# Four attention layers on one core: residual kept in SBUF, attention outputs stored once as float32, accumulator copy and value products reordered, other DMA steps

## The chip, the cores and the metric

The kernel runs on one core of one Trainium2 chip. The metric is the device time of one execution in microseconds (us). Three runs of the kernel before took 6309.92, 6320.90 and 6321.18 us, so the median is 6320.9 us. The profile comes from one further execution, which took 6320.79 us; its span, from the first to the last instruction in the profile, is 6319.0 us.

## The reference

```python
def _A_ref(x, wqkv, wo):                     # 32 heads of width 18, S = 2048, D = 576
    qkv = (x @ wqkv).reshape(B, S, 3, H, Dh).transpose(2, 0, 3, 1, 4)
    q, k, v = qkv[0], qkv[1], qkv[2]
    scores = jnp.einsum("bhqd,bhkd->bhqk", q, k) * (Dh ** -0.5)
    o = jnp.einsum("bhqk,bhkd->bhqd", _softmax(scores), v)
    return o.transpose(0, 2, 1, 3).reshape(B, S, D) @ wo
# _B_ref: the same with one k and one v of width 18 that all 32 heads share

x = A_x
x = x + _A_ref(_layernorm(x), A_wqkv, A_wo)
x = x + _B_ref(_layernorm(x), B_wq, B_wk, B_wv, B_wo)
x = x + _A_ref(_layernorm(x), A_wqkv, A_wo)
x = x + _B_ref(_layernorm(x), B_wq, B_wk, B_wv, B_wo)
```

All inputs and the output are float32. Where the kernel multiplies in the faster matmul format `F32R`, it splits a float32 number into a rounded part `hi` and a remainder `lo` and adds up the products of the parts (`TERMS`, 14 products for a contraction over 576).

## The kernel before

**Four layers, each in four stages.** (1) *Projection*: 8 blocks `tt` of 256 tokens. The normalized rows are transposed and split (`trans`, `split_rows`) into a tile `xt`, and `project` makes q and k, which go to DRAM (`qk_d`). (2) *Attention*, the long stage. (3) *Output projection* (`out_proj`): 16 chunks `c` of 128 tokens; `out_w` makes 28 matmuls (14 for each half of 288 columns, tile `psn`) and adds the result to the residual. (4) The normalization for the next layer, woven into (3).

**Attention** runs over groups: a group is one pair of heads `p` (16 of them) and one block `u` of 512 queries (4 of them), so 64 groups in a layer and 256 in all. A group takes 8 steps `st` of 4 slots `i`. The row maxima of a group are made first (`max_mm`: PE fills a two-bank tile `psm`, VectorE reduces it at line 439), and `LEAD` = 14 steps later come the scores again, transposed, with the maximum subtracted in the matmul (`exp_mm`: PE fills `pse`, one of three banks, and ScalarE takes the exponential into a tile `pt`), and then the products with the values (`pv_block`). `max_mm` and `exp_mm` of one slot use different halves of the PE rows. A `pv_block` of one step multiplies four `pt` tiles with the values into one PSUM bank, `oacc`; each logical product is two matmuls in the profile. In slot 1 the second half (256 columns) of the step before last is multiplied, in slot 3 the first half of the last step. The first step of a group is the exception (`pv_slot`): its first half is left out in slot 3, and all 512 columns are done in slot 1 of the next step, because `oacc` must be copied (`oc`, line 576, on ScalarE) before the next group overwrites it. The copy stands in ScalarE's order behind the exponential of slot 1.

**Work around a group.** A table `todo` says at which step each piece is issued; every engine has its own order and only waits for what it needs. For group `g`, with `b` its last step of maxima:

- The maxima are finished (`max_final`: VectorE line 528, then three small GpSimd instructions), turned (`max_store` at `b`+2: VectorE line 538, four DMAs at line 540 into `m_d`) and laid as two rows into the q tile (`max_rows` at `b`+5: two DMAs at line 544). The scores of the group need these rows.
- The sum of the exponentials comes from the copy `oc`: `o_sum` (three GpSimd instructions, lines 132 and 590), `l_part` (line 595: two DMAs, `lt`), `l_inv` (line 599, VectorE), `l_out` (line 602, to `r_d`), `l_rows` (line 607, `rb`), `o_mul` (GpSimd line 612, then two more that make `hi` and `lo`, lines 132 and 615), `o_out` (line 621, four DMAs into `o_d`).

All DMAs are issued in one order by SyncE (SP), and SP waits at each for what it depends on. With 8 steps in a group, pieces of several groups fall on the same step; where they do, the older group's come first. Counted modulo 8, the phases are: `max_store` 1, `max_rows` 4, `o_sum` 0, `l_part` 1, `l_inv` and `l_out` 4, `l_rows` 6, `o_mul` 0, `o_out` 2. So at phase 0 GpSimd gets `o_mul` of an older group ahead of `o_sum`; at phase 1 SP gets `l_part` ahead of `max_store`; at phase 4 it gets `l_out` ahead of `max_rows`.

**Output projection.** The residual lies in DRAM (`x_d`, or the input in layer 0). `load_res` brings each chunk into a tile `xr`, `out_w` adds into it, and a DMA (line 297) stores it; `load_x` loads it again for the next layer's normalization. `out_rows` loads `hi` and `lo` of the attention outputs for 256 tokens straight into a matmul operand `ot` (three buffers). What is left of the last groups' steps is run between the chunks (`run_tail`, two steps a chunk).

Of the kernel before, what the change touches and what calls it, by code (L numbers as in the profile page):

```python
# [8 lines left out]
F32 = mybir.dt.float32  # L9
# [9 lines left out]
P = 128  # L19
# [28 lines left out]
L_AT = 4  # L48
INV_AT = 7
R_AT = 7  # L50
RB_AT = 9
MUL_AT = 11
O_AT = 13
# [10 lines left out]
XT = 3  # L64
# [3 lines left out]
def tile_kernel(ctx: ExitStack, tc: tile.TileContext, A_x, A_wqkv, A_wo, B_x, B_wq, B_wk, B_wv, B_wo, out):  # L68
# [24 lines left out]
    wsm = cst.tile([P, 10, D], F32R, name="wsm")  # L93
    vbuf = cst.tile([P, NCH * H * (DH + 1)], F32, name="vbuf")
# [8 lines left out]
    o_d = dram.tile([2, D, S], F32, name="o_d")  # L103
    r_d = dram.tile([H, S], F32, name="r_d")

    rbs = [cst.tile([P, 512], F32, name=f"rb{i}") for i in range(2)]
# [4 lines left out]
    for t in rbs + sums + [h_.bitcast(F32) for h_ in hls]:  # L111
        nc.gpsimd.memset(t, 0.0)
    x_d = [dram.tile([S, D], F32, name=f"x_d{i}") for i in range(2)]
# [11 lines left out]
    def ptile(name, shape=(P, 512), dt=F32):  # L125
        return pool.tile(list(shape), dt, tag="p", bufs=16, name=name)
# [87 lines left out]
    xcs, xrs = {}, {}  # L214

    def load_x(tt, src):
        for c in (2 * tt, 2 * tt + 1):
            xcs[c] = pool.tile([P, D], F32, tag="xc", bufs=4, name="xc")
            nc.sync.dma_start(xcs[c], src[c * P:(c + 1) * P, :])

    def stats(c):
        xc = xcs[c]
# [10 lines left out]
    def scaled(c, mv, rs):  # L233
        xc = xcs.pop(c)
# [14 lines left out]
    def load_res(c, src):  # L249
        if c < NCH:  # L250
            xrs[c] = pool.tile([P, D], F32, tag="xr", bufs=4, name="xr")
            nc.sync.dma_start(xrs[c], src[c * P:(c + 1) * P, :])

    def out_w(c):
        ot = ots_[c // 2][:, :, c % 2 * P:(c % 2 + 1) * P]
        for h in range(2):
            cs = slice(h * 288, (h + 1) * 288)
            nc.vector.tensor_tensor(xrs[c][:, cs], natural(ot, h, mtile), xrs[c][:, cs], op=OP.add)  # L258

    ots_, lts, rls, his = {}, {}, {}, {}  # L260
    xhs, xts = {}, {}

    def trans(c):
        tt, u = divmod(c, 2)
        if u == 0:
            xts[tt] = pool.tile([P, 9, 256], F32R, tag="xt", bufs=XT, name="xt")
# [16 lines left out]
    def out_proj(x_res_prev, x_new_prev):  # L283

        for c in range(2):
            load_res(c, x_res_prev)
        yield -1
        for c in range(NCH + 1):
            if c < NCH:
# [424 lines left out]
```

## Time and profile before

| | |
|---|---|
| median of three runs | 6320.9 us (6309.92 to 6321.18) |
| the profiled execution: time, span | 6320.79 us, 6319.0 us |
| mean granted TensorE clock over it | 0.979 |
| VectorE busy | 5323.0 us (84%) |
| ScalarE busy | 4691.3 us (74%) |
| GpSimd busy | 1815.4 us (29%) |
| moved by DMA | 359.38 MB, 57 GB/s on average |

How to read it: PE is TensorE's matmuls and PEld its weight loads, DVE is VectorE, ACT ScalarE, POOL GpSimd; SPq is SyncE's queue of DMA issues. `pse<-big` means that an instruction reads the tile `big` and writes the tile `pse`. A row of the timeline shows the start and the duration of one instruction, or of several alike that follow each other (x8), and in brackets the idle time of the engine before it with what ended it. Matmuls are pipelined: the next starts before the recorded end of the one before, so the distance of starts says more than a duration.

### The profile page before, as it was taken

To read this page: it belongs to the slowest core of one execution; us is meant where nothing else is said; L and a number is where in the kernel's file an instruction comes from. 1 tells how busy PE (TensorE), PEld (TensorE's weight loads), DVE (VectorE), ACT (ScalarE), POOL (GpSimd) and SP (SyncE) were. 2 spreads that over 40 slices of the span, in tenths; PEclk is the share of its full clock that TensorE was granted. 3 is DMA by queue.
4 is the path that set the end of the run, shared out by engine and by line. 5 is a ranking of instruction groups with operands and counts; after the bars stand their busy time and mean duration, and the time that the engine had idled before them with its cause. 6 is when DMAs were issued, how large, how long until landed. Compare 5 with 4: busy or idle time off the path is not lost.

```text
span 6319.0 us, 134168 instructions
## 1 busy us (share of the span) xinstructions
PE 6064.2 (96%) x53280; PEld 2682.3 (42%) x53280; DVE 5323.0 (84%) x5592; ACT 4691.3 (74%) x8848; POOL 1815.4 (29%) x2701
## 2 busy tenths in 40 slices
PE   9999999999899999999899999999998999999999
PEld 8533333334733333333595333333347333333335
DVE  4799999996589999999337999999964999999992
ACT  2588888887178888888425888888861788888883
POOL 2132322333123323333311332333330233332331
PEclk9999999999999999999999999999998999999998
DMA  5311111112611111011453111111126111011004
GB/s 188 93 46 36 32 36 36 33 33 60 205 48 24 24 25 23 23 25 24 142 178 87 42 35 36 34 35 36 30 75 192 46 25 25 24 25 25 22 16 129
DMA packets 348700, 359.38 MB, mean 57 GB/s; under 512 B 142776, under 2 KB 283376, under 8 KB 338352
## 3 DMA queue, kind: packets, MB, share of 16 engines
q1 hardware_dynamic: 348072, 350.81, 19.8%
q8 instruction: 419, 6.86, 0.5%
q14 instruction: 209, 1.71, 0.1%
HBM read 201.05 MB, written 145.59 MB: 55 GB/s over the span
## 4 chain that ended last, share of the span: by engine, by line
PE 55%; DVE 14%; DMA 8%; POOL 7%; ACT 7%; SPq 6%; issue 4%; POOLq 0%; DVEq 0%; ACTq 0%
PE pse L553 23%; PE oacc L570 20%; DVE mx L439 13%; PE psq L322 5%; ACT pt L556 5%; PE psn L209 4%; DMA big<-m_d 3%; PE psm L433 3%; SPq L540 2%; ACT oc L576 2%; SPq L621 1%; POOL oh L615 1%; POOL os L590 1%; POOL os L132 1%; DMA x_d<-xr 1%
## 5 line engine op out<-in xcount | busy, mean ns | idle before, releaser
L439 DVE TENSOR_REDUCE mx<-psm 128x1 f32<-128x1024 f32 x4096 | 4971.0, 1219 | 273.8 <-PE psm L433 258.5
L556 ACT ACTIVATE pt<-pse 128x512 f32<-128x512 f32 x8192 | 4428.8, 600 | 752.8 <-PE psm L433 331.1
L433 PE MATMUL psm<-big 62*128 62x512 f32 x8192 | 3065.8, 453 | 48.2 <-DVE mx L439 39.2
L553 PE MATMUL pse<-big 64*128 64x512 f32 x8192 | 3000.0, 446 | 116.4 <-DMA big<-m_d 74.8
L570 PE MATMUL oacc<-pt,vbuf 128*19 128x256 f32 (+1 forms) x30720 | 2534.9, 402 | 0.0
L553 PEld LDWEIGHTS pse<-big 64*128 64x128 f32 x8192 | 1233.6, 185 | 1981.1 <-ACT pt L556 1897.1
L433 PEld LDWEIGHTS psm<-big 62*128 62x128 f32 x8192 | 1232.2, 187 | 150.5 <-DVE mx L439 130.9
L570 PEld LDWEIGHTS oacc<-pt,vbuf 128*19 128x19 f32 x30720 | 523.1, 97 | 1380.1 <-issue 1375.8
L530 POOL TENSOR_SCALAR neg<-mm 128x8 f32<-128x8 f32 x256 | 50.9, 199 | 3263.8 <-DVE mm L528 3263.8
L322 PE MATMUL psq<-xt,big 128*128 128x256 f32 (+1 forms) x3136 | 427.8, 297 | 26.0 <-DVE ev L332 17.3
L322 PEld LDWEIGHTS psq<-xt,big 128*128 128x128 f32 (+1 forms) x3136 | 407.7, 201 | 44.1 <-DVE ev L332 20.3
L326 ACT ACTIVATE ev<-psq 128x512 fp32r<-128x512 f32 (+2 forms) x148 | 73.2, 495 | 446.4 <-PE psq L322 401.4
L612 POOL TENSOR_TENSOR os<-os,rb 96x512 f32<-96x512 f32 x256 | 327.5, 1279 | 113.2 <-DMA rb<-r_d 101.6
L132 POOL TENSOR_SCALAR os<-oc 32x512 f32<-32x512 f32 x512 | 316.0, 617 | 66.2 <-ACT oc L576 28.2
L615 POOL TENSOR_TENSOR oh<-os,oh 96x512 fp32r<-96x512 f32 x256 | 327.9, 1281 | 21.4
L590 POOL TENSOR_TENSOR os<-os,oc 96x512 f32<-96x512 f32 x256 | 327.8, 1280 | 21.4
L209 PE MATMUL psn<-wsm,ot 128*128 128x288 f32 x1792 | 263.6, 310 | 49.4 <-DVE xr L258 49.4
L258 DVE TENSOR_TENSOR xr<-psn,xr 128x288 f32<-128x288 f32 x128 | 56.4, 454 | 270.2 <-PE psn L209 124.1
L209 PEld LDWEIGHTS psn<-wsm,ot 128*128 128x128 f32 x1792 | 256.0, 201 | 58.4 <-DVE xr L258 55.7
L332 DVE TENSOR_TENSOR ev<-psq,ev 128x512 fp32r<-128x512 f32 (+2 forms) x120 | 69.7, 591 | 199.8 <-ACT ev L326 187.0
L193 ACT ACTIVATE xt<-ps 128x512 fp32r<-128x512 f32 x64 | 38.2, 596 | 215.7 <-PE ps L201 214.9
L576 ACT ACTIVATE oc<-oacc 128x512 f32<-128x512 f32 x256 | 154.4, 603 | 23.0 <-PE oacc L570 23.0
(52 smaller groups left out, 1239.7 us busy)
## 6 DMA issues: line engine op xcount, KB each, us to landing
big<-qk_d SPq DMA_DIRECT2D x180, 432.0 KB
qk_d<-ev SPq DMA_DIRECT2D x192, 256.0 KB
o_d<-oh SPq DMA_DIRECT2D x1024, 36.0 KB
ot<-o_d SPq DMA_DIRECT2D x64, 512.0 KB
qk_d<-ev SPq DMA_DIRECT2D x240, 128.0 KB
rb<-r_d SPq DMA_DIRECT2D x512, 36.0 KB
m_d<-tr SPq DMA_DIRECT2D x1024, 2.0 KB
x_d<-xr SPq DMA_DIRECT2D x48, 288.0 KB
```

Of the source, the lines that this page charges most:

```text
L132: eng.tensor_scalar(dst, src, 1.0, 0.0, op0=OP.mult, op1=OP.add)
L209: nc.tensor.matmul(ps, lhs[:, xc, :], wsm[:, wc, h * 288:(h + 1) * 288], start=i == 0, stop=i == len(TERMS) - 1)
L322: nc.tensor.matmul(ps[:n, k, :], w[:, wc, :n], xt[:, xc, :], start=j == 0, stop=j == len(TERMS) - 1)
L433: nc.tensor.matmul(ps[:, i % 2], q[b:b + KM, c0:c0 + P], k[b:b + KM, kb * 512:(kb + 1) * 512], start=True, stop=True)
L439: nc.vector.reduce_max(mxs[p, u][:, a * 4 + qc, j // 8:j // 8 + 1], ps.rearrange("p a t -> p (a t)"), axis=AX.X)
L553: nc.tensor.matmul(e, k[r:r + KE, kc * P:(kc + 1) * P], q[r:r + KE, u * 512:(u + 1) * 512], start=True, stop=True)
L556: nc.scalar.activation(pt, e, AF.Exp, scale=SCALE)
L570: nc.tensor.matmul(oacc[j:j + DH + 1, cs], v[:, kc, 2 * p + a if is_a else 0, :], pts[p, u, i][:, cs], start=kc < 2, stop=kc >= 14 and hal ...
L576: nc.scalar.activation(oc, oacc, AF.Copy)
L590: nc.gpsimd.tensor_tensor(t[:96], t[:96], oc[:96], op=OP.add)
L612: nc.gpsimd.tensor_tensor(t[:96], t[:96], rbs[u % 2][:96], op=OP.mult)
L615: nc.gpsimd.tensor_tensor(lo[:96], t[:96], hi.bitcast(F32)[:96], op=OP.subtract)
```

## The change

1. **Residual.** One tile `xo` of 16 x 576 floats a partition holds the whole residual. It is loaded once from the input in layer 0; `stats`, `scaled` and `out_w` work on slices of it. `load_res`, the tiles `xc` and `xr`, the DRAM tensors `x_d`, their stores and the reloads are gone. In the last layer each chunk is stored to the output from `xo`. The next layer's first normalization steps move from chunks 4 and 5 to chunks 3 and 4.
2. **Attention outputs.** `o_mul` is one GpSimd instruction instead of three, and `o_out` two DMAs instead of four: `o_d` holds float32. `out_rows` loads it into three tiles from the pool of `pt`, and the new `out_t` makes `hi` (copies on ScalarE, for the first block on VectorE) and `lo` (subtractions on VectorE) in the operand `ot`. `ot` and `xt` have two buffers instead of three, the pool of `pt` 15 instead of 16, `rb` one instead of two.
3. **Copy and value products.** In the step in which a group's last value product is issued, the exponential of slot 1 is issued after the copy `oc` instead of before it. `pv_slot` is gone: each step's products are done in halves, the first step of a group too, whose first half now stands in slot 3, half a step behind the copy. The flag `start` is set on the first half alone.
4. **Order.** New distances, and with them the phases modulo 8: `o_sum` stays at 0, `l_part` goes to 2, `l_inv` and `l_out` to 5, `l_rows` to 0, `o_mul` to 2, `o_out` to 4. `max_store` (1) and `max_rows` (4) stay.

```diff
-L_AT = 4
-INV_AT = 7
-R_AT = 7
-RB_AT = 9
-MUL_AT = 11
-O_AT = 13
+L_AT = 5
+INV_AT = 8
+R_AT = 8
+RB_AT = 11
+MUL_AT = 13
+O_AT = 15
...
+    xo = cst.tile([P, NCH, D], F32, name="xo")
...
     def out_rows(tt):
         ts = slice(tt * 256, tt * 256 + 256)
-        ots_[tt] = pool.tile([P, 9, 256], F32R, tag="xt", bufs=XT, name="ot")
-        ot = ots_[tt].bitcast(F32)
+        ors[tt] = t = [ptile("o", (P, 2, 256)) for _ in range(3)]
         for i in range(2):
-            nc.sync.dma_start(ot[:, 5 * i:5 * i + 4], o_d[i, :512, ts].rearrange("(c p) t -> p c t", p=P))
-            nc.sync.dma_start(ot[64 * i:64 * i + 64, 4], o_d[i, 512:, ts])
+            nc.sync.dma_start(t[i], o_d[256 * i:256 * i + 256, ts].rearrange("(c p) t -> p c t", p=P))
+            nc.sync.dma_start(t[2][64 * i:64 * i + 64, 0], o_d[512:, ts])
+
+    def out_t(tt, hi):
+        ots_[tt] = ot = pool.tile([P, 9, 256], F32R, tag="xt", name="ot")
+        ot_f = ot.bitcast(F32)
+        t = ors.pop(tt)
+        for i in range(2):
+            copy(hi, ot[:, 2 * i:2 * i + 2], t[i])
+            nc.vector.tensor_tensor(ot[:, 5 + 2 * i:7 + 2 * i], t[i], ot_f[:, 2 * i:2 * i + 2], op=OP.subtract)
+        copy(hi, ot[:, 4], t[2][:, 0])
+        nc.vector.tensor_tensor(ot[64:, 4], t[2][64:, 0], ot_f[64:, 4], op=OP.subtract)
 
     def out_w(c):
         ot = ots_[c // 2][:, :, c % 2 * P:(c % 2 + 1) * P]
         for h in range(2):
             cs = slice(h * 288, (h + 1) * 288)
-            nc.vector.tensor_tensor(xrs[c][:, cs], natural(ot, h, mtile), xrs[c][:, cs], op=OP.add)
+            nc.vector.tensor_tensor(xo[:, c, cs], natural(ot, h, mtile), xo[:, c, cs], op=OP.add)
...
+    def out_proj(last):
+
+        for c in range(NCH):
+            tt = c // 2
+            if c >= OUT_AHEAD:
+                run_tail(TAIL)
+            if c % 2 and tt + 2 < 8:
+                out_rows(tt + 2)
+            out_w(c)
+            if c % 2 == 0 and tt + 1 < 8:
+                out_t(tt + 1, nc.scalar)
+            if last:
+                nc.sync.dma_start(y_out[c * P:(c + 1) * P, :], xo[:, c])
+            yield c
...
-            pt = ptile("pt")
-            nc.scalar.activation(pt, e, AF.Exp, scale=SCALE)
-            pts[p, u, i] = pt
+
+            def finish():
+                pt = pts[p, u, i] = ptile("pt")
+                nc.scalar.activation(pt, e, AF.Exp, scale=SCALE)
+            return finish
...
-            cs = slice(0, 512) if half is None else slice(half * 256, half * 256 + 256)
+            cs = slice(half * 256, half * 256 + 256)
...
-                                 start=kc < 2, stop=kc >= 14 and half == 1)
+                                 start=kc < 2 and half == 0, stop=kc >= 14 and half == 1)
...
         def o_mul(p, u):
             t = sums[u % 2]
-            nc.gpsimd.tensor_tensor(t[:96], t[:96], rbs[u % 2][:96], op=OP.mult)
-            hi, lo = his[p, u] = [pool.tile([P, 512], F32R, tag="oh", name="oh") for _ in range(2)]
-            copy(nc.gpsimd, hi[:96], t[:96])
-            nc.gpsimd.tensor_tensor(lo[:96], t[:96], hi.bitcast(F32)[:96], op=OP.subtract)
+            nc.gpsimd.tensor_tensor(t[:96], t[:96], rb[:96], op=OP.mult)
...
-        for i in range(XT - 1):
-            at(b - 8 + 2 * i + 4 * (i // 2), out_rows, i)
+        at(b - 5, out_rows, 0)
+        at(b - 2, out_t, 0, nc.vector)
+        at(b - 1, out_rows, 1)
...
             for i in range(4):
+                held = None
                 if 0 <= se < ns:
-                    exp_mm(*divmod(se // STEPS, 4), se % STEPS * 4 + i, st >= ns)
+                    held = exp_mm(*divmod(se // STEPS, 4), se % STEPS * 4 + i, st >= ns)
+
+                    if i != 1 or (se - 2) % STEPS != STEPS - 1:
+                        held()
+                        held = None
...
                 if i == 1:
-                    pv_slot(se - 2, 1)
+                    pv_block(se - 2, 1)
                 elif i == 3:
-                    pv_slot(se - 1, 0)
+                    pv_block(se - 1, 0)
+                if held:
+                    held()
```

More of the change, by code (lines that the diff above doesn't have):

```diff
@@ L281, in run_tail @@
                     f(*args)
[L283 to L289, printed above, removed]
[L290 to L303 removed]
+    def out_proj(last):
[11 more added lines that the diff above has]
+            yield c
+        assert not tail and not ors
+    load_x(0)
     for layer in range(4):
         is_a = layer % 2 == 0
[L306 to L307 removed]
         if is_a:
@@ L484, in tile_kernel @@
                     load_wsm(c, A_wqkv[:, 2 * D:])
-            if tt < 5:
-                load_x(tt + 3, x_res)
+            if layer == 0 and tt < 5:
+                load_x(tt + 3)
             gs = groups if tt < 6 else first
@@ L676, in tile_kernel @@
                 tail = [todo.pop(n, []) for n in range(ns + LEAD + L_AT + 1, ns + LEAD + O_AT)]
-                outs = out_proj(x_res, x_new)
-                next(outs)
+                outs = out_proj(layer == 3)
             elif ns <= se < ns + OUT_AHEAD:
```

73 lines of the change are left out of this document (23 added, 50 removed).

## The prediction

> **What bounds the kernel now.** I read the page first, then the timeline of a few steps in the long stage, then the waits, then the distances of the copies `oc`, which count groups, and last the four output projections.
>
> ```profile
> PE 6064.2 (96%) x53280; PEld 2682.3 (42%) x53280; DVE 5323.0 (84%) x5592; ACT 4691.3 (74%) x8848; POOL 1815.4 (29%) x2701
> L439 DVE TENSOR_REDUCE mx<-psm 128x1 f32<-128x1024 f32 x4096 | 4971.0, 1219 | 273.8 <-PE psm L433 258.5
> ```
>
> Three engines look full, so the page alone does not say which one sets the pace. The timeline does:
>
> ```profile
> 1006.93 0.50 PE L553 MATMUL pse<-big 64*128 64x512 f32 x1
> 1007.26 0.39 PE L553 MATMUL pse<-big 64*128 64x512 f32 x1
> 1007.59 0.63 PE L570 MATMUL oacc<-pt,vbuf 128*19 128x256 f32 x8
> 1017.94 0.49 PE L553 MATMUL pse<-big 64*128 64x512 f32 x1
> 3447.89 9.35 DVE L439 TENSOR_REDUCE mx<-psm 128x1 f32<-128x1024 f32 x8
> ```
>
> Half a step on PE is a pair of scores (with its pair of maxima beside it), 0.33 us later the second pair, 0.33 us later the value products, and then the next half. From 1006.93 to 1017.94 lie nine halves: 11.01 / 9 = 1.22 us. VectorE can go faster: the last row is a stretch after it was held up, in which eight reductions took 9.35 us; with the last one's own 1.22 us off, seven distances are 8.13 us, 1.16 each. So in the regular state PE sets 1.22 us, and the reductions follow it. A group without any hold-up would take 16 x 1.22 = 19.52 us.
>
> **Two losses in each group.** The first stands where the copy is made:
>
> ```profile
> 1002.86 0.49 PE L553 MATMUL pse<-big 64*128 64x512 f32 x1
> 1003.15 0.60 ACT L576 ACTIVATE oc<-oacc 128x512 f32<-128x512 f32 x1
> 1003.43 0.39 PE L553 MATMUL pse<-big 64*128 64x512 f32 x1
> 1003.62 2.09 ACT L556 ACTIVATE pt<-pse 128x512 f32<-128x512 f32 x4
> 1004.29 0.49 PE L553 MATMUL pse<-big 64*128 64x512 f32 x1
> 1004.72 1.06 PE L570 MATMUL oacc<-pt,vbuf 128*19 128x512 f32 x8
> 1005.70 0.50 PE L553 MATMUL pse<-big 64*128 64x512 f32 x1
> ```
>
> Two halves should take 2.44 us; from 1002.86 to 1005.70 it is 2.84, a loss of 0.40. PE runs ahead (no value products in the first half), then has to wait for exponentials that stand behind the copy, and then does 512 columns at once.
>
> The second is the way of the maxima to the scores:
>
> ```profile
> 1005.90 1.28 POOL L612 TENSOR_TENSOR os<-os,rb 96x512 f32<-96x512 f32 x1
> 1007.65 0.20 DVE L538 STREAM_TRANSPOSE tr<-hl 128x32 f32<-128x32 f32 x1
> 1007.98 1.28 POOL L615 TENSOR_TENSOR oh<-os,oh 96x512 fp32r<-96x512 f32 x1
> 1010.73 1.28 POOL L590 TENSOR_TENSOR os<-os,oc 96x512 f32<-96x512 f32 x1
> 1012.03 1.13 SPq L595 DMA_DIRECT2D lt<-os  x2
> 1013.22 1.96 SPq L540 DMA_DIRECT2D m_d<-tr  x4
> 1015.23 1.40 SPq L621 DMA_DIRECT2D o_d<-oh  x4
> 1017.74 0.70 SPq L544 DMA_DIRECT2D big<-m_d  x2
> 1019.64 0.46 PE L553 MATMUL pse<-big 64*128 64x512 f32 x1 [0.41 <-ACT pt L556]
> ```
>
> The turned maxima are ready at 1007.85, but SP stores them at 1013.22: ahead of that store stands `l_part`, which waits for `o_sum` on GpSimd, and that for the three instructions of `o_mul`. The rows come at 1017.74, end their issue at 1018.44, and the scores that need them start at 1019.64. The bracket names ScalarE, but its work was done; the waits of the whole run name the DMA, and the same lateness for `lt`:
>
> ```profile
> PE pse L553 <- DMA big<-m_d: 74.8, 101, 2.4
> DVE rl L599 <- DMA lt<-os: 103.5, 30, 17.5
> SPq L595 <- POOL os L590: 2754.0, 230, 16.5
> ```
>
> What both cost is read from the copies, 64 in each layer, and from one group at the start that has no such wait:
>
> ```profile
> L576 ACT ACTIVATE oc<-oacc x64: 599/603/605, 263.7 to 1566.0; 128x512 f32<-128x512 f32 x64
> L576 ACT ACTIVATE oc<-oacc x64: 597/603/604, 1793.0 to 3084.8; 128x512 f32<-128x512 f32 x64
> L576 ACT ACTIVATE oc<-oacc x64: 599/604/605, 3414.4 to 4712.8; 128x512 f32<-128x512 f32 x64
> L576 ACT ACTIVATE oc<-oacc x64: 597/603/604, 4946.9 to 6245.8; 128x512 f32<-128x512 f32 x64
> L576 ACT ACTIVATE oc<-oacc x2: 603/603/603, 263.7 to 283.6; 128x512 f32<-128x512 f32 x2
> ```
>
> The undisturbed group takes 19.9 us, which is 19.52 + 0.40. The four layers take 1302.3 + 1291.8 + 1298.4 + 1298.9 = 5191.4 us for 4 x 63 = 252 groups, 20.60 each. So 252 x 19.92 = 5020 is regular, and 171 us are waits of the second kind with what follows from them. Some of it is a slow clock:
>
> ```profile
> 6210.40:6241.00 30.60, 30.60 (x154) 9.29 (x148) 0.20 (x1) 16.31 (x31) 8.57 (x9) 0.50 0.53 157
> ```
>
> Here (columns: PE, weight loads, VectorE, ScalarE, GpSimd, granted clock, DMA share, GB/s) the clock was 0.50 for 30.6 us, a loss of 15.
>
> **The change, part by part.**
>
> *Order of the steps.* With `o_sum` alone at phase 0, GpSimd does it straight after the finishing of the maxima: in the rows above it could start at 1005.9 and end 2.6 us later, at 1008.5. SP has `max_store` first: from 1007.85, four issues, to about 1009.9. `l_part` follows, to 1011. At phase 4 stand `o_out`, ready since `o_mul` (one instruction of 1.28 us, done by 1010), 0.7 us for two issues, and `max_rows`: about 1012 to 1013 instead of 1017.74, landed by 1014.2. The scores need them near 1019, so 4 to 5 us are to spare. `l_inv` moves a step later (2.4 us) while `lt` comes a microsecond earlier, so VectorE no longer waits for it. `l_rows` now precedes `max_store` on SP, but waits only for a store made some 6 us before. I take 25 of the 171 us as staying (0.1 a group, for weight loads that share GpSimd and for the clock), so **-146**. Bounds: 0, if something else makes the rows late, and -171.
>
> *Copy and halves.* The last value product's recorded end, some 0.2 us before the copy at 1003.15, allows it to start only about 0.1 earlier, because the wait across engines costs 0.1 or more. It would run from 1003.07 to 1003.67. The new half of products is due at 1002.86 + 0.66 = 1003.52, and now waits for the copy, to about 1003.77; what is queued behind it on PE, all scores and maxima, waits too. One 0.56 later the next half starts (1004.33); its second pair needs an exponential that two others and the copy precede, 1004.7; then 0.33 + 0.56 to 1005.6. That is 0.1 less than 1005.70. Bounds: no loss at all, -0.40, and +0.1 where each wait costs as much again. I take -0.1: 252 x 0.1 = **-25**, from -101 to +25. That ScalarE does the held exponential 0.5 us later costs nothing by itself: its score bank is needed a half later.
>
> The Trainium skill, in "PSUM — Partial Sum Buffer", section "PSUM bank collisions raise a hardware error", says that two engines on one bank and the same partitions must be kept apart by semaphores, whatever columns they touch. This is the rule that speaks against the change: half the columns do not help, the product must wait for the whole copy. If one took it the other way, as if the first 256 columns were free after half the copy, the loss would go nearly to nothing.
>
> *Residual and outputs.* The four output projections, first to last start, and a stretch of four chunks that did not wait:
>
> ```profile
> L209 PE MATMUL psn<-wsm,ot x448: 288/295/445, 1561.3 to 1639.2; 128*128 128x288 f32 x150
> L209 PE MATMUL psn<-wsm,ot x448: 288/295/609, 3080.1 to 3165.9; 128*128 128x288 f32 x150
> L209 PE MATMUL psn<-wsm,ot x448: 288/295/442, 4708.1 to 4790.0; 128*128 128x288 f32 x150
> L209 PE MATMUL psn<-wsm,ot x448: 288/295/610, 6241.1 to 6315.0; 128*128 128x288 f32 x150
> 4712.61 15.07 PE psn L209 x112
> PE psn L209 <- DVE xr L258: 49.4, 21, 4.9
> L195 DVE TENSOR_TENSOR xt<-ps,xt 128x512 fp32r<-128x512 f32 x64 | 43.9, 687 | 60.3 <-ACT xt L193 60.2
> ```
>
> 77.9 + 85.8 + 81.9 + 73.9 = 319.5 us. Four chunks take 15.07, so 16 take 60.3; with the last value products and transposes 62, in the last layer 61: 247 in all. The 72 us above that are the residual's late loads, which hold VectorE's additions and so PE. With the residual in SBUF nothing is loaded. Added for each pair of chunks (7.5 us): on ScalarE two copies of 0.60 and a smaller one, on VectorE two subtractions of 0.69 and a smaller one, beside two to four additions of about 0.46. Both are covered by PE, since `out_t` for the next pair stands after the first chunk of this one; without the cover a pair would cost 3.5 us. The loads (0.64 MB) are issued a pair earlier. I leave 1 us a layer: **-68**, from 0 to -72. `out_t(0)` on VectorE falls into steps without reductions: nothing. Fewer loads elsewhere: -2.
>
> Sum from the profiled execution's own time: 6320.8 - 146 - 25 - 68 - 2 = **6080 us**. That execution is 0.1 us from the median.
>
> **The rivals.**
>
> - *VectorE takes over* (0.12). By its recorded durations a group costs it 16 x 1.219 and three small instructions of about 0.20 (line 538's), 20.10 us, so the groups could gain only 252 x (20.60 - 20.10) = 126 in place of 171: 6320.8 - 126 - 70 = 6125. Against it stand the reductions 1.16 us apart. The Trainium skill, in "Perfetto Trace Analysis", section "Identifying the Most-Contended Engine", calls matmul busy time a poor measure and VectorE's occupancy a fair one; by that rule the 84% would be the bound, and this rival the forecast.
> - *The output operand takes the residual's place* (0.12). The three `o` tiles, the copies and the subtractions come late with two `ot` buffers; the 68 us are given back: 6148.
> - *The rows stay late* (0.11): not SP's order, but another transfer on the way sets them. Then the change does not do what its steps say: 6320.8 - 25 - 70 = 6226.
> - *Slower* (0.05). `max_rows` now stands behind `o_out` on SP, and `o_out` behind the whole chain sum, reciprocal, rows, `o_mul`. If that is ready only later than about 17 us after the copy, each group waits; 0.96 us a group uses up the 241 us of the sum. At 1.5 us: 6080 + 378 = 6458. For it: SP waits 2754 us at `l_part` today, so such waits are real. Against: `o_mul` would be done 5 us ahead.
> - *More than forecast* (0.07): the copy's loss goes too, 6080 - 76 = 6004.
>
> **How the numbers follow.** My forecast has 0.53. Its own range is 6050 to 6110. The range from 6020 to 6180 takes in the first two rivals and leaves out the next two and half of the last. A change of 0.2%, 13 us, can be told from none; all cases but the slow one are faster by more: faster 0.93, same 0.02, slower 0.05.
>
> **What would show it.** Copies 19.8 us apart nearly everywhere; line 540's DMAs before line 595's, no wait of PE for `big<-m_d`, none of VectorE for `lt`; from the half before the copy to the second one behind it about 2.75 us; 448 output matmuls in about 62 us. Wrong would be groups at 20.1 or more, line 544 waiting behind line 621, or gaps before `psn`.

## The result and the profile after

| | before | after |
|---|---|---|
| median of 4 runs each | 6315.41 us (6304.52 to 6321.18) | 6066.76 us (6065.49 to 6072.54) |
| the profiled execution | 6320.79 us, span 6319.0 | 6067.45 us, span 6065.7 |
| mean granted clock | 0.979 | 0.988 |

The ratio is 0.961, with a 95% interval of 0.9593 to 0.9627. Between the two profiled executions lie 253.3 us. The copies `oc` and the output matmuls tell in which stages. First the copies of the kernel after, from its view of one tile, the 64 of each layer (shortest, median and longest duration in ns, then first and last start):

```profile
L572 ACT ACTIVATE oc<-oacc x64: 597/598/601, 261.2 to 1516.7; 128x512 f32<-128x512 f32 x64
L572 ACT ACTIVATE oc<-oacc x64: 597/597/599, 1728.1 to 2979.9; 128x512 f32<-128x512 f32 x64
L572 ACT ACTIVATE oc<-oacc x64: 597/598/601, 3281.9 to 4540.7; 128x512 f32<-128x512 f32 x64
L572 ACT ACTIVATE oc<-oacc x64: 597/597/599, 4752.6 to 6004.5; 128x512 f32<-128x512 f32 x64
```

and the matmuls of its four output projections, from the same kind of view:

```profile
L208 PE MATMUL psn<-wsm,ot x448: 288/295/400, 1511.9 to 1575.3; 128*128 128x288 f32 x150
L208 PE MATMUL psn<-wsm,ot x448: 288/295/445, 2975.2 to 3041.6; 128*128 128x288 f32 x150
L208 PE MATMUL psn<-wsm,ot x448: 288/295/400, 4536.0 to 4599.4; 128*128 128x288 f32 x150
L208 PE MATMUL psn<-wsm,ot x448: 288/294/402, 5999.7 to 6061.7; 128*128 128x288 f32 x150
```

| part of the span | before | after | difference | forecast |
|---|---|---|---|---|
| groups, first to last copy of each layer, added up | 5191.4 | 1255.5 + 1251.8 + 1258.8 + 1251.9 = 5018.0 | -173.4 | -146 - 25 = -171 |
| output projections, first to last start | 319.5 | 63.4 + 66.4 + 63.4 + 62.0 = 255.2 | -64.3 | -68 |
| all else | | | -15.6 | -2 |

The last line is the rest of the 253.3. Half of it lies between the second and the third layer: from the last copy of the one to the first of the other were 3414.4 - 3084.8 = 329.6 us and are 302.0 now, 27.6 less, of which the projection has 85.8 - 66.4 = 19.4. One piece of the other 8.2 is a wait of PE for the evicted `ev`, 5.52 us in the trace before (at 3187.91) and 1.74 in the one after (at 3059.84).

A group now takes 19.85 us nearly everywhere; 252 of them are 5002, and the 16 us above that are the last group of each layer (21.55, it holds the loads of the weights for the projection) and one group of 22.95 and one of 26.37 in the first and third layers. There the weights of the next layer are loaded, and PE has its two last waits for rows of maxima.

The page of the kernel after says who is busy (microseconds, share of the span; in a group's row the time busy, the mean ns of one, and the idle time before them):

```profile
PE 5973.7 (98%) x55328; PEld 2633.7 (43%) x55328; DVE 5413.5 (89%) x5700; ACT 4757.8 (78%) x8932; POOL 1332.8 (22%) x2188
PE 92%; ACT 3%; DVE 2%; POOL 1%; DMA 1%; issue 1%; SPq 1%; POOLq 0%; DVEq 0%; ACTq 0%
L434 DVE TENSOR_REDUCE mx<-psm 128x1 f32<-128x1024 f32 x4096 | 4974.0, 1220 | 113.0 <-PE psm L428 79.2
```

The second row is the chain of work that ended last: 92% of what set the end is PE's own work. The page of the kernel before has this row as

```profile
PE 55%; DVE 14%; DMA 8%; POOL 7%; ACT 7%; SPq 6%; issue 4%; POOLq 0%; DVEq 0%; ACTq 0%
```

The third row of the page after is the one that read 273.8 us of idle time before: VectorE's reductions stand idle 161 us less, and of that idle time the part that ends with PE's maxima fell from 258.5 to 79.2 us. The list of waits of the same run (engine, tile and line that wait, what they wait for, us in sum, times, longest):

```profile
PEld oacc L566 <- ACT oc L572: 123.4, 252, 0.5
DVE rl L589 <- DMA lt<-os: 34.4, 11, 5.3
PE pse L546 <- DMA big<-m_d: 5.5, 2, 2.9
PE psn L208 <- DVE xo L258: 5.2, 4, 2.2
```

The first is new: in every one of the 252 groups with a successor, the weight loads for the first half of the value products wait for the whole copy. The second was 103.5. The third is all that is left of PE's waits for the rows `m_d`, 5.5 us where 74.8 stood; the fourth is what is left of PE's waits for the additions in the output projections, 5.2 us where 49.4 stood.

The place of the copy, from the timeline of the kernel after (start, duration, engine, line; a bracket gives the idle time and who ended it):

```profile
995.75 0.49 PE L546 MATMUL pse<-big 64*128 64x512 f32 x1
995.88 0.60 ACT L572 ACTIVATE oc<-oacc 128x512 f32<-128x512 f32 x1 [0.23 <-PE oacc L566]
996.53 0.14 PEld L566 LDWEIGHTS oacc<-pt,vbuf 128*19 128x19 f32 x8 [0.49 <-ACT oc L572]
997.09 0.50 PE L546 MATMUL pse<-big 64*128 64x512 f32 x1
997.51 0.49 PE L546 MATMUL pse<-big 64*128 64x512 f32 x1
997.93 0.63 PE L566 MATMUL oacc<-pt,vbuf 128*19 128x256 f32 x8
998.50 0.50 PE L546 MATMUL pse<-big 64*128 64x512 f32 x1
```

From 995.75 to 998.50 are 2.75 us for two halves, where 2.84 stood. Without any loss the products would start 0.66 after the half, at 996.41; they start at 996.53, which is 0.12 for the copy. (The 0.49 in that row is idle time of the weight loads, which stand idle for 0.37 ahead of the products of an ordinary half too.) The second pair comes 0.42 behind the first instead of 0.33 (997.09 to 997.51): the trace has it wait for ScalarE, whose exponentials stand behind the copy. The products follow that pair by 0.42 too (997.93), and there the trace names no wait; in another run below a pair that stands alone takes 0.43 as well. These three, 0.12 and twice 0.09, make 0.30 of the 0.31.

GpSimd's `neg` and SP's order of a group, from the timeline of the kernel after:

```profile
998.06 0.20 POOL L523 TENSOR_SCALAR neg<-mm 128x8 f32<-128x8 f32 x1 [15.10 <-DVE mm L521]
1000.67 1.70 SPq L533 DMA_DIRECT2D m_d<-tr  x4
1002.41 1.13 SPq L585 DMA_DIRECT2D lt<-os  x2
1003.64 0.80 SPq L607 DMA_DIRECT2D o_d<-os  x2
1004.63 0.52 SPq L537 DMA_DIRECT2D big<-m_d  x2
```

The first small GpSimd instruction of this group is `neg`, the first row here, and the rows are fetched 6.6 us later (1004.63). In the kernel before, the timeline has it at

```profile
1005.18 0.20 POOL L530 TENSOR_SCALAR neg<-mm 128x8 f32<-128x8 f32 x1 [13.38 <-DVE mm L528]
```

and line 544 at 1017.74, 12.6 us later. Groups of several kernels are laid beside each other by that instruction below.

### The profile page after: what moved, and what is told of

The parts are those of the page before. It is cut to its first block, busy times and chain, and to the rows that moved or that the text cites. A ratio compares the mean times of both kernels' runs of the same rounds, so it can differ in the third digit from the quotient of the medians.

```text
span 6065.7 us, 136534 instructions
## 1 busy us (share of the span) xinstructions
PE 5973.7 (98%) x55328; PEld 2633.7 (43%) x55328; DVE 5413.5 (89%) x5700; ACT 4757.8 (78%) x8932; POOL 1332.8 (22%) x2188
## 4 chain that ended last, share of the span: by engine, by line
PE 92%; ACT 3%; DVE 2%; POOL 1%; DMA 1%; issue 1%; SPq 1%; POOLq 0%; DVEq 0%; ACTq 0%
PE pse L546 41%; PE oacc L566 38%; PE psn L208 5%; PE psq L317 5%; PE psm L428 3%; ACT oc L572 3%; DVE mx L434 1%; DVE ev L327 0%; POOL rs L226 0%; DMA big<-qk_d 0%; PE ps L200 0%; DMA raw<-in_A_wqkv_dram 0%; POOL wsm L153 0%; DMA qk_d<-ev 0%; DVE st L221 0%
## 5 line engine op out<-in xcount | busy, mean ns | idle before, releaser
L434 DVE TENSOR_REDUCE mx<-psm 128x1 f32<-128x1024 f32 x4096 | 4974.0, 1220 | 113.0 <-PE psm L428 79.2
L546 PE MATMUL pse<-big 64*128 64x512 f32 x8192 | 3040.1, 448 | 5.5 <-DMA big<-m_d 5.5
L566 PE MATMUL oacc<-pt,vbuf 128*19 128x256 f32 x32768 | 2575.8, 386 | 13.5
L566 PEld LDWEIGHTS oacc<-pt,vbuf 128*19 128x19 f32 x32768 | 557.3, 97 | 1498.6 <-issue 1373.5
L208 PE MATMUL psn<-wsm,ot 128*128 128x288 f32 x1792 | 243.3, 297 | 5.2 <-DVE xo L258 5.2
L208 PEld LDWEIGHTS psn<-wsm,ot 128*128 128x128 f32 x1792 | 239.9, 189 | 9.8 <-ACT ot L129 4.5
L258 DVE TENSOR_TENSOR xo<-psn,xo 128x288 f32<-128x288 f32 x128 | 57.8, 454 | 151.5 <-PE psn L208 150.7
L129 ACT ACTIVATE ot<-o 128x512 fp32r<-128x512 f32 (+1 forms) x84 | 41.9, 553 | 140.4 <-PE psn L208 101.3
L208 PE MATMUL psn<-wsm,xt 128*128 128x288 f32 x896 | 125.0, 295 | 0.0
```

What stands on the lines that cost most here:

```text
L208: nc.tensor.matmul(ps, lhs[:, xc, :], wsm[:, wc, h * 288:(h + 1) * 288], start=i == 0, stop=i == len(TERMS) - 1)
L434: nc.vector.reduce_max(mxs[p, u][:, a * 4 + qc, j // 8:j // 8 + 1], ps.rearrange("p a t -> p (a t)"), axis=AX.X)
L546: nc.tensor.matmul(e, k[r:r + KE, kc * P:(kc + 1) * P], q[r:r + KE, u * 512:(u + 1) * 512], start=True, stop=True)
L566: nc.tensor.matmul(oacc[j:j + DH + 1, cs], v[:, kc, 2 * p + a if is_a else 0, :], pts[p, u, i][:, cs], start=kc < 2 and half == 0, stop=kc ...
```

## The experiments

All times are medians; each ratio is to the kernel before, run on the same chip beside it, and its 95% interval is about 0.0015 to either side. "Group" is the second layer's mean, first to last copy over 63: 20.50 us before, 19.87 after.

### The order alone, and the change in the old order

**Order alone**: the kernel before with the six distances of the change.

```diff
-L_AT = 4
-INV_AT = 7
-R_AT = 7
-RB_AT = 9
-MUL_AT = 11
-O_AT = 13
+L_AT = 5
+INV_AT = 8
+R_AT = 8
+RB_AT = 11
+MUL_AT = 13
+O_AT = 15
```

> The kernel before with nothing but the six new distances (residual in DRAM, hi and lo stored, three GpSimd instructions in o_mul, copy behind the exponential). If SP's and GpSimd's order made the rows of the maxima late, groups fall from 20.60 to about 19.93 us (16 halves of 1.22 and the 0.40 at the copy) and the time to about 6170 us, with no wait of PE for big<-m_d. If the length of o_mul or another transfer made them late, groups stay above 20.3 us and the time above 6260 us.

Measured: 6174.89 us, ratio 0.978; group 19.95; the four layers' groups add up to 5047.0 us, 144.4 less than before; the projections keep 316.4. The waits of this run for the rows:

```profile
PE pse L553 <- DMA big<-m_d: 13.7, 4, 5.0
```

Four waits in place of 101. So the new order is enough by itself, and is worth what the forecast gave it.

**Old order**: the change, with the same six lines turned round.

```diff
-L_AT = 5
-INV_AT = 8
-R_AT = 8
-RB_AT = 11
-MUL_AT = 13
-O_AT = 15
+L_AT = 4
+INV_AT = 7
+R_AT = 7
+RB_AT = 9
+MUL_AT = 11
+O_AT = 13
```

> The changed kernel with the six old distances. If the order is what was needed, the waits come back and with them some 146 us: about 6210 us. Rival: o_mul is two instructions (1.9 us) shorter and o_out two DMAs (0.7 us) shorter than before, so even in the old order the rows come 2 us or more earlier than before, where they were late by 0.5 us in a typical group; then groups stay at 19.85 us and the time below 6090 us.

Measured: 6078.19 us, ratio 0.9629; group 19.87; a single wait of PE for `m_d` in the whole run, of 1.2 us. The rival held: given the rest of the change, the order is worth 11 us. SP in this run, from its timeline:

```profile
1002.43 1.13 SPq L585 DMA_DIRECT2D lt<-os  x2
1003.60 1.97 SPq L533 DMA_DIRECT2D m_d<-tr  x4
1005.62 0.69 SPq L607 DMA_DIRECT2D o_d<-os  x2
1008.33 0.73 SPq L537 DMA_DIRECT2D big<-m_d  x2
```

The store of the maxima stands behind `l_part` again, but GpSimd has one instruction of `o_mul` to do ahead of `o_sum` instead of three, and `o_out` issues two DMAs instead of four. `neg` of this group starts at 997.65, so the rows are fetched 10.7 us after it: later than with the new order (6.6), earlier than in the kernel before (12.6), and early enough.

### How late the rows may be

**Old order, long `o_mul`**: two more GpSimd instructions of the old kind into a scratch tile, which nobody reads, and the six old distances; one buffer less for the exponentials.

```diff
-O_AT = 15
+O_AT = 13
...
             nc.gpsimd.tensor_tensor(t[:96], t[:96], rb[:96], op=OP.mult)
+            oh = pool.tile([P, 512], F32R, tag="oh", bufs=1, name="oh")
+            copy(nc.gpsimd, oh[:96], t[:96])
+            nc.gpsimd.tensor_tensor(oh[:96], t[:96], oh.bitcast(F32)[:96], op=OP.subtract)
```

> The changed kernel in the old order (as e2) with two GpSimd instructions added behind o_mul that make hi and lo into a scratch tile nobody reads, so that o_mul takes 3.2 us of GpSimd again; one output store as in the change; 14 buffers instead of 15. If e2 stayed fast because o_mul is short, the rows are late again: groups 20.1 to 20.5 us and 6150 to 6230 us. If the two output DMAs fewer on SP did it, the time stays within 20 us of e2's 6078.

Measured: 6124.51 us, ratio 0.9708, between the two expectations; group 20.01, with many at 19.85 and others from 20.1 to 21.1. From the list of waits of this run:

```profile
PE pse L546 <- DMA big<-m_d: 21.4, 39, 2.4
```

One of its groups, from the timeline:

```profile
1001.88 0.20 POOL L523 TENSOR_SCALAR neg<-mm 128x8 f32<-128x8 f32 x1 [13.05 <-DVE mm L521]
1009.90 2.79 SPq L533 DMA_DIRECT2D m_d<-tr  x4
1014.29 0.63 SPq L537 DMA_DIRECT2D big<-m_d  x2
```

With a store of the maxima that took 2.79 us to issue, the rows were fetched 12.4 us after `neg`. So some groups wait and others do not: this kernel stands on the edge. Two GpSimd instructions in each group are worth 46 us in the old order (6124.5 against 6078.2; what the missing buffer has in it was not tried apart, but with 11 buffers and the new order the group below takes 19.87). That is a third of the 140 us that the late rows cost in the kernel before; the other step that was longer there, `o_out` with four issues instead of two, is what the next run was for.

**Hi and lo, old order**: the next kernel below (residual in SBUF, all output stores and loads of before) with the old distances, to see what the two extra stores of `o_out` are worth.

```diff
-MUL_AT = 13
-O_AT = 15
+MUL_AT = 11
+O_AT = 13
...
```

> e9 (residual in SBUF, hi and lo stored and loaded as before, copy and halves as in the change) in the old order: o_mul has three instructions on GpSimd again and o_out four DMAs on SP. It differs from e10 by the two output stores that follow each group. If the rows come late as soon as both queues carry their old load in the old order, the waits of before are back: groups about 20.4 us, 252 x 0.55 = 140 us more than the change, about 6210 us. If GpSimd's part alone sets it, the time stays near e10's 6125.

Measured: 6390.18 us, ratio 1.0112, 1.1% slower than the kernel before. A miss (about 6210 or 6125 was expected), and of no use for its question:

```profile
ACT pt L552 <- POOL os L581: 402.8, 247, 2.4
PE pse L547 <- ACT pt L552: 223.3, 244, 1.7
```

These are two lines of its waits. To make room this kernel has 11 buffers for exponentials instead of 15, and the copy `oc` holds one of them until `o_sum` has read it. The old order puts `o_sum` behind `o_mul`, so the exponentials wait for GpSimd in 247 groups. With the new order the same 11 buffers do (below). What the two extra stores cost stays open.

### The copy and the halves, each alone

**Old copy**: the change with the first products of a group in 512 columns, and the exponential not held.

```diff
-            if not 0 <= n < ns:
+            if not 0 <= n < ns or (half == 0 and n % STEPS == 0):
                 return
...
-            cs = slice(half * 256, half * 256 + 256)
+            one = n % STEPS == 0
+            cs = slice(0, 512) if one else slice(half * 256, half * 256 + 256)
...
-                                 start=kc < 2 and half == 0, stop=kc >= 14 and half == 1)
+                                 start=kc < 2 and one, stop=kc >= 14 and half == 1)
...
-                    held = exp_mm(*divmod(se // STEPS, 4), se % STEPS * 4 + i, st >= ns)
-
-                    if i != 1 or (se - 2) % STEPS != STEPS - 1:
-                        held()
-                        held = None
+                    exp_mm(*divmod(se // STEPS, 4), se % STEPS * 4 + i, st >= ns)()
```

> The changed kernel with copy and value products as before (copy behind the exponential, a group's first products in one go of 512 columns). By the forecast's working a group's copy loses 0.40 us again instead of 0.31: groups 19.93 us, 252 x 0.09 = 23 us more, about 6090 us. Rival: the halves save nothing, 6067 us; or the copy cost more than one group shows, over 6110 us.

Measured: 6091.66 us, ratio 0.965, group 19.95. The two parts together are worth 24.9 us in the change.

**Halves alone**: the last piece of that diff (the exponential is not held), nothing else.

> The changed kernel with the halves, but the exponential of slot 1 issued before the copy, as before. If the start of the copy decides, the copy starts 0.1 us later or a little more, the first half of products waits that much longer: groups about 19.95 us, about 6092 us. If the copy's start is set by the last value product anyway, no change: 6067 us.

Measured: 6069.53 us (6062.12 to 6070.46), ratio 0.9612, group 19.84. A miss: I had expected to lose what the copy's place brings, and it brings nothing. From the waits of this run:

```profile
PEld oacc L566 <- ACT oc L572: 161.5, 252, 0.6
PE oacc L566 <- ACT oc L572: 51.5, 251, 0.2
```

The weight loads of the products do wait longer for the copy (161.5 us against 123.4), and now the products themselves do too (51.5). But the exponential that is no longer held is ready earlier for the scores behind it. One copy of this run's timeline shows both: its half starts at 992.97, and the products come at

```profile
993.91 0.63 PE L566 MATMUL oacc<-pt,vbuf 128*19 128x256 f32 x8 [0.20 <-ACT oc L572]
```

That is 0.94 behind the half, 0.28 later than without a loss (0.12 in the change). From there on every piece keeps its regular distance, the second pair 0.33 behind the first, the products 0.33 behind that, and the second half ends at 995.69: 2.72 us for the two halves against 2.75. The two come out even.

**Copy ahead alone**: the diff of "old copy" without its last piece, so the exponential is held.

> The changed kernel with the copy ahead of the exponential, but a group's first products in one go of 512 columns. The held exponential frees its score bank at 1.1 us after the copy's start, where PE, with nothing to multiply meanwhile, needs it at 0.5: PE waits, then does 512 columns at once. Loss at the copy about 0.7 us instead of 0.31, 252 x 0.4 = 100 us more, about 6170 us. Rival: order on ScalarE alone does not matter, 6067 to 6090 us.

Measured: 6185.98 us, ratio 0.9799; group 20.32, as the copies show:

```profile
L573 ACT ACTIVATE oc<-oacc x64: 597/597/598, 1760.6 to 3040.9; 128x512 f32<-128x512 f32 x64
```

(3040.9 - 1760.6) / 63 = 20.32. With 512 columns in one go the hold costs 94 us against "old copy". The four kernels make a square:

| | exponential first | copy first |
|---|---|---|
| 512 columns | 6091.66 | 6185.98 |
| halves | 6069.53 | 6066.76 |

### The residual and the outputs, each alone

**Residual in DRAM**: the change, but the residual is stored and loaded as before.

```diff
+            load_res(c + 2, x_res_prev)
             out_w(c)
...
+            if c > 0:
+                nc.sync.dma_start(x_new_prev[(c - 1) * P:c * P, :], xrs.pop(c - 1))
```

> The changed kernel with the residual in DRAM again, loaded for each chunk and stored, and loaded once more for the normalization. If the residual's loads made the output projections long, these go from 64 back to about 80 us from the first to the last matmul, and the time to about 6135 us. If the hi and lo of the attention outputs (twice the bytes) were it, they stay near 65 us and the time below 6085 us.

Measured: 6101.77 us, ratio 0.9666, between the two. The projections take 70.6 + 75.6 + 72.2 + 63.9 = 282.3 us, and PE waits 24.8 us for the additions in them (49.4 before, 5.2 after); the second of them, which is 85.8 before and 66.4 after:

```profile
L208 PE MATMUL psn<-wsm,ot x448: 288/295/577, 2986.3 to 3061.9; 128*128 128x288 f32 x150
```

**Hi and lo**: the residual in SBUF, but the outputs split by GpSimd and stored and loaded twice as before (four DMAs in `o_out`, three operand buffers, no `out_t`, 11 buffers for exponentials), in the new order.

```diff
-    o_d = dram.tile([D, S], F32, name="o_d")
+    o_d = dram.tile([2, D, S], F32, name="o_d")
...
+            hi = rb.bitcast(F32R)
+            his[p, u] = rb, t
+            copy(nc.gpsimd, hi[:96], t[:96])
+            nc.gpsimd.tensor_tensor(t.bitcast(F32R)[:96], t[:96], rb[:96], op=OP.subtract)
```

> The changed kernel with the residual in SBUF, but hi and lo of the attention outputs stored and loaded as before (four DMAs in o_out, three GpSimd instructions, three operand buffers, no out_t; 11 buffers in the pool of the exponentials). If the residual's loads alone were late before, the output projections stay near 255 us in sum. If the bytes of hi and lo share the blame, as e7's 282 suggests, they come to 270 to 290 us. Attention itself may be a little slower with 11 buffers; its groups should stay below 20 us.

Measured: 6079.46 us (6075.23 to 6086.08), ratio 0.9631; group 19.87; the projections take 62.4 + 69.0 + 62.3 + 62.5 = 256.2 us. One of them:

```profile
L210 PE MATMUL psn<-wsm,ot x448: 288/294/406, 1515.3 to 1577.7; 128*128 128x288 f32 x150
```

So the residual in SBUF alone takes nearly all of the projections' gain (319.5 to 256.2). The single output load alone, as "residual in DRAM" has it, takes a good half (to 282.3), and both together no more than the first. Here too either part removes waits that the other would remove as well.

### Three attempts at what is left

**Products earlier**: halves alone, and the last half of a group's products one pair earlier, so that the copy can start sooner.

```diff
-                if i == 1:
+                if i == (0 if (se - 2) % STEPS == STEPS - 1 else 1):
                     pv_block(se - 2, 1)
```

> The changed kernel with one more move: in the step of the copy the last half of value products is issued in slot 0, ahead of the second pair of scores, not in slot 1, so the copy starts 0.33 us earlier. If the wait of the first half for the copy, with what follows from it, is the 0.31 us a group that is left, it goes: groups 19.54 to 19.65 us, 5990 to 6015 us. If the score banks behind the copy hold PE instead, the time stays within 15 us of 6067.

Measured: 6100.09 us, ratio 0.9664, group 19.97: slower than the change by 33 us. PE, the copy and a reduction in the timeline of this run:

```profile
559.03 0.63 PE L566 MATMUL oacc<-pt,vbuf 128*19 128x256 f32 x8
559.72 0.60 ACT L572 ACTIVATE oc<-oacc 128x512 f32<-128x512 f32 x1
560.15 2.36 DVE L434 TENSOR_REDUCE mx<-psm 128x1 f32<-128x1024 f32 x2 [0.75 <-PE psm L428]
560.49 0.63 PE L566 MATMUL oacc<-pt,vbuf 128*19 128x256 f32 x8
561.05 0.49 PE L546 MATMUL pse<-big 64*128 64x512 f32 x1
561.43 0.50 PE L428 MATMUL psm<-big 62*128 62x512 f32 x1
```

The copy is over at 560.32, and the products start at 560.49, 0.32 behind the pair at 560.17 as in any half: the copy no longer delays them. But the products now part the two pairs that fill one tile of maxima. In the rows above the scores at 561.05 have no maxima beside them (elsewhere each pair has both); those come 0.38 later, at 561.43. VectorE was idle for 0.75 us and then has two reductions back to back, to 562.5; a tile comes free only as the first of them ends, at about 561.3, which is when those maxima start.

**Half later**: halves alone, and the first half of a group's products one pair later instead.

```diff
+                if i == 0 and (se - 2) % STEPS == 0:
+                    pv_block(se - 2, 0)
-                if i == 1:
+                elif i == 1:
                     pv_block(se - 2, 1)
-                elif i == 3:
+                elif i == 3 and (se - 1) % STEPS:
                     pv_block(se - 1, 0)
```

> The changed kernel with the exponential not held, and with the first half of a group's first products issued a quarter of a step later, in slot 0 of the next step between the two pairs of scores, so that the copy is done when PE comes to it, and neither scores nor maxima come in bunches. If the wait for the copy is what is left of the loss (0.31 us a group), groups fall to 19.55 to 19.65 us and the time to 5995 to 6020 us. If value products between the two pairs are what made e6 slow, whatever the spacing, it is slower than 6067.

Measured: 6102.74 us, ratio 0.9665, group 19.95. Also a miss, and alike: three pairs stand in a row, and the third has to wait for a tile of maxima (timeline of this run):

```profile
560.96 0.40 PE L546 MATMUL pse<-big 64*128 64x512 f32 x1
561.24 0.50 PE L428 MATMUL psm<-big 62*128 62x512 f32 x1
561.67 0.63 PE L566 MATMUL oacc<-pt,vbuf 128*19 128x256 f32 x8
562.23 0.50 PE L546 MATMUL pse<-big 64*128 64x512 f32 x1
562.66 0.63 PE L566 MATMUL oacc<-pt,vbuf 128*19 128x256 f32 x8
```

The pair that is left between two blocks of products takes 0.43 (562.23 to 562.66) where one of two neighbours takes 0.33.

**Halves, late loads**: halves alone, and the weights of the next layer split in the second half of the projection.

```diff
-                if is_a and 2 <= c < 7:
-                    load_a(c - 2, (1,))
+                if is_a and 9 <= c < 14:
+                    load_a(c - 9, (1,))
```

> The changed kernel with two edits: the exponential is not held (e4, where groups took 19.81 instead of 19.85 us), and the weight loads that the output projection of layer 1 carries are issued in chunks 9 to 13 instead of 2 to 6, so that the small GpSimd instructions of the next normalization no longer wait behind their DMAs. 252 x 0.03 = 8 us and 4 us at chunks 5 and 6: 6055 us. If what e4 gained in the groups is lost elsewhere, as its time of 6069.5 says, and the loads are as late at their new place, no change from 6067.

Measured: 6064.44 us (6058.06 to 6070.09), ratio 0.9595. The second layer's projection goes from 66.4 to 63.8 us, 2.6 of the 4 us that were expected. The 6055 did not come: the whole is 2 us below the change, which these runs cannot tell from nothing. No kernel here beats the change by a difference that can be told.

## Why the prediction was right

Forecast 6080 us, measured 6067 (profiled execution and median alike). Point by point:

- **PE sets the pace: right.** An undisturbed group was put at 19.92 before and 19.82 after. "Old copy" and "order alone" show 19.95 for the first, the change 19.85 to 19.87 for the second. The rival in which VectorE takes over needed 20.10, and groups that are faster than its recorded durations allow refute it; the two attempts to move the products show that its reductions, at two tiles of maxima, are not far behind. The Trainium skill, "Perfetto Trace Analysis", section "Identifying the Most-Contended Engine", has the engine of the highest occupancy as the one to speed up first, with VectorE's occupancy as a fair measure. The trace does not bear that out here: VectorE rose from 84% to 89%, yet its reductions still stood idle 79.2 us for PE's maxima, and 92% of the chain is PE.
- **Order of the steps: the size right (-146 forecast, -140 in time and -144 in the groups measured), the attribution half right.** The step followed the new order through GpSimd and SP, and each place came out: store ahead of `l_part`, rows fetched 6.6 us after `neg` (the forecast's 1012 to 1013 is 6.8 to 7.8 after the 1005.18), none of the regular groups waiting for rows, and VectorE waiting for `lt` 11 times instead of 30 (none was forecast). What the step did not see is that the rest of the change removes the same wait by itself: with it the old order costs 11 us. The gain belongs to either, not to their sum. The shorter `o_mul` is shown to have a part in this (46 us in "old order, long `o_mul`"); the part of the shorter `o_out` is argued, as the run for it met another wait. That 25 us of the 171 would stay was about right in size: 16 did, in the groups that load weights. The clock, which was to be in them, went almost wholly (table at the end). The rival in which the rows stay late is out with this.
- **Copy and halves: -25 forecast, -24.9 measured as the pair**, and 2.75 us for the two halves as forecast. That the figures meet so closely is luck, for two places of the working were off. The first is that the copy ahead of the exponential helps a little: by the square above the halves make the gain, and the copy's place makes nothing with them and costs 94 us without them. The second is the share of each half. Counted from the start of the half, the copy was put at 0.21, the products at 0.91 and the second half at 1.47; they came at 0.13, 0.78 and 1.34, since the waits across engines cost less than the 0.1 that was taken (the copy ends at 996.48, the products start at 996.53). The second half was put at 1.27 and took 1.41, as its pair and its products both came 0.42 behind the one ahead, where 0.37 and 0.33 were taken. The case of more than forecast did not come: the copy still loses 0.31.
- **The product waits for the whole copy: right.** The wait stands in all 252 groups (0.49 us of idle weight loads each, 0.12 us of delay for the products in the group shown), though the first half touches 256 columns only. This is what the Trainium skill's "PSUM — Partial Sum Buffer", "PSUM bank collisions raise a hardware error", asks for, and the trace agrees. What the group would take if half the copy were enough was not run.
- **Residual and outputs: -68 forecast, -64.3 measured**; three projections at 62 to 63.4 us, and 66.4 in the one where GpSimd has weights to split. The size and the wait were right, the account was too narrow in two ways. The residual's loads are not the whole cause: with them put back, and the outputs still loaded once, only 27 of the 64 us return. And some 20 of the 64 us are not waits at all: the output matmuls themselves are busy 263.6 us before and 243.3 after, at a granted clock of 0.90 to 0.96 before and 0.97 to 1.00 after. The rival in which the output operand takes the residual's place did not come: with both `out_t` copies in, chunks stay covered.
- **The slower rival** (line 537 behind `o_out` on SP) did not come: the four rows of SP's timeline above follow each other within 4.5 us, and the rows are fetched 6.6 us after `neg`, where the scores need them about 14 after it (1005.18 to 1019.64 in the trace before, less the 0.4 of lateness).
- **Elsewhere: the term that was mis-sized**, -2 against -15.6. It is nearly the whole of the 13 us between forecast and time. 8.2 us of it lie between the second and third layers, where one wait is 3.8 us shorter. The other runs separate it: without the projection this stretch takes 242.2 to 245.1 us in the three kernels that have the residual in DRAM (before, "order alone", "residual in DRAM") and 234.5 to 237.8 in all eleven that have it in SBUF (the change and ten runs). "Residual in DRAM" alone differs from the change by 6.6 us there. So most of the 8.2 goes with the residual's stores and reloads, where the forecast took 2 us for all loads. The other 7 us are spread over the start and the other two layer changes, which differ by as much between kernels that are alike there; they stay open.

## What to carry to other kernels

When a late result stands behind a queue's head, a new order and a shorter head are two cures of one wait: count the time from the first to the last step of the handover in each variant, and do not add the two gains. Read the pace of a pipeline from the distances of one repeating instruction, not from the busy shares of the engines. A residual that stayed on chip freed a stage by itself. Splitting work into halves paid here (22 us), where an engine otherwise had to finish a long piece behind a wait, while moving pieces in between neighbours that fill one buffer cost 31 to 33 us, more than the wait it removed. And when waits go, look at the granted clock too: part of the gain can lie in it.

## What the hardware showed that was not expected

Recorded durations overstate what VectorE needs. In the last layer's groups the windows of the kernel after (length, then busy time and count for PE, weight loads, VectorE, ScalarE, GpSimd, then granted clock, DMA share, GB/s) are:

```profile
4755.00:5995.00 1240.00, 1236.73 (x11958) 437.70 (x11950) 1205.47 (x1168) 1110.01 (x2064) 286.07 (x458) 1.00 0.09 21
```

By its records VectorE is busy for 1205.47 of 1240 us, 97%, and by 16 recorded reductions and three small instructions a group would take it 20.10 us; groups take 19.85. Neighbouring records overlap (1.16 us apart where one reads 1.22), so a share of 97% was not the bound.

The clock goes with the waits. What the granted clock fell short of 1.00, added up over windows of 10 us, and the output matmuls beside it (us):

| | clock, groups | clock, output projections | output matmuls busy | PE's waits for the additions |
|---|---|---|---|---|
| before | 29.0 | 20.4 | 263.6 | 49.4 |
| order alone | 5.1 | 17.0 | 261.5 | 47.9 |
| residual in DRAM | 3.4 | 6.8 | 250.7 | 24.8 |
| after | 1.7 | 1.7 | 243.3 | 5.2 |

"Order alone" takes the waits out of the groups, and the clock recovers there and not in the projections; in each stage the shortfall falls with the waits. A part of what the change gained, some 27 us in the groups and 19 in the projections as an upper estimate from this table, is by this estimate clock and not idle time. The stretch at 0.50 of 30.6 us in the kernel before (from 6210.40) began 2 us behind a short wait of PE there, from its timeline:

```profile
6208.12 0.73 PE L553 MATMUL pse<-big 64*128 64x512 f32 x2 [1.06 <-DMA big<-m_d]
```

A wait of 1.06 us preceded 15 us of loss. Not every such wait is followed by one: after a wait of 1.67 us at 771.97 the clock was at 0.50 for about 3.4 us, after one of 1.16 us at 814.74 it stayed at 1.00. In the kernel after, whose groups have almost no such waits, the window above has 1.00 throughout. Whether the waits bring the slow clock about was not tried apart from all else.
